# Attention with head dim 192: scores as one full 128-row part and a remainder on two 64-row tiles

## Chip, cores, metric

The kernel runs on one core of a Trainium2 chip. The metric is the device time of one execution in microseconds.

Names: PE is TensorE, PEld its weight loads, ACT is ScalarE, DVE is VectorE, POOL is GpSimd, SP is the queue that issues the DMAs. "Head" is one of the 16 x 32 = 512 independent attention problems; four heads are a group and are loaded together.

## The reference

```
B, H, Sq, Sk, D = 16, 32, 368, 512, 192        # bf16
scores = einsum("bhqd,bhkd->bhqk", q, k) * D**-0.5
p      = softmax(scores, axis=-1)
out    = einsum("bhqk,bhkd->bhqd", p, v)
```

## The kernel before

For each head, PE transposes K (it is loaded with keys on partitions), DVE copies it out of PSUM (the K eviction), PE makes the scores transposed (keys on partitions, 368 queries in the free dimension), ACT takes exp into `pt`, PE multiplies `pt` with V, which has two extra columns of ones that give the softmax denominator, and DVE and ACT divide. Q arrives transposed by the DMA. The 192 head dims are contracted in two blocks of 96 rows.

The parts that matter (cuts marked `...`):

```python
DH = 96; NC = 4; NPAIR = 2                      # 4 chunks of 128 keys, 2 pairs of chunks
st    = ps("st", [128, NC, 512], FP32)          # scores, in PSUM: one buffer only
o_ps  = ps("o_ps", [128, NM, 512], FP32)        # output, NM = 3
tk_ps = ps("tk_ps", [128, 2, 512], BF16)        # transposed K
...
def qk(n, j):                                   # PE: one HALF of a head's scores
    ...
    if n >= 1:
        pe.wait_ge(sem_act, NPAIR * (n - 1) + j + 1)   # this half of exp(n-1) is done
    for c in (2 * j, 2 * j + 1):
        for blk in range(2):
            ins = pe.matmul(st[:, c, 0:SQ],
                lhsT=kt_sb[0:DH, kb, blk, c * 128:(c + 1) * 128],
                rhs=qt[0:DH, sl, blk, h * SQ:(h + 1) * SQ],
                start=(blk == 0), stop=(blk == 1))
    ins.then_inc(sem_st, 1)
...
for i in range(-1, NH + 1):                     # PE's order of work
    qk(i, 0); pv(i - 1, 0); t_k(i + 1); qk(i, 1); pv(i - 1, 1); pv(i - 1, 2)
...
for j in range(NPAIR): exp_pair(i, j)           # ACT: one exp for each half
norm_last(i - 1)                                # ACT: divides the last third of the output
```

`st` exists once, but it is handed to ACT and back in two halves. While ACT works on one half, PE works on the other.

The softmax here doesn't subtract the row's maximum and nothing guards it: scores larger than these inputs give would overflow.

Of the kernel before, what the change touches and what calls it, by code (L numbers as in the profile page):

```python
# [11 lines left out]
def bass_standalone__gqa_softmax__near_ridge_kernel(  # L12
# [14 lines left out]
    assert SQ <= 512 and SQ % 16 == 0  # L27
# [3 lines left out]
    DH = 96  # L31
    VW = D + 2

    MCH = []
    s0 = 0
    while s0 < SQ:
        MCH.append((s0, min(128, SQ - s0)))
        s0 += 128
    NM = len(MCH)
    assert NM == 3, "PSUM plan assumes 3 query chunks"  # L40

    HPD = 1
    for cand in (4, 2):
        if NH % cand == 0 and rep == 1:
            HPD = cand
            break
    NG = NH // HPD
# [10 lines left out]
    with ExitStack() as es:  # L58
# [13 lines left out]
        qt = sb("qt", [128, NBG, 2, HPD * SQ], BF16)  # L72
        v_pad = sb("v_pad", [128, 3, NC, VW], BF16)
        kt_sb = sb("kt_sb", [128, 2, 2, SK], BF16)
# [7 lines left out]
        tk_ps = ps("tk_ps", [128, 2, 512], BF16)  # L82
# [8 lines left out]
        sem_dve = sem("sem_dve")  # L91
        sem_vp = sem("sem_vp")
        sem_k = [sem(f"sem_k{i}") for i in range(NBG)]
# [6 lines left out]
        O_DMAS = NM  # L100

        q_exp = []
        _acc = [0] * NBG
        for _g in range(NG):
            _acc[_g % NBG] += 16 * (2 + (1 if _g == NG - 1 else 0))
            q_exp.append(_acc[_g % NBG])
# [5 lines left out]
        def _(sp):  # L112
            def q_dmas(g):
                return 2 + (1 if g == NG - 1 else 0)

            def loads(g):
                sl = g % NBG
                n0 = g * HPD
                last = g == NG - 1
                if g >= NBG:  # L120
                    gp = g - NBG
                    last_head = gp * HPD + HPD - 1
                    sp.wait_ge(sem_tk, last_head + 1)
                    sp.wait_ge(sem_vp, last_head + 1)
                    sp.wait_ge(sem_st, NPAIR * (last_head + 1))
                R = HPD * SQ
                for blk in range(2):
                    col0 = blk * DH
                    nrows = R - 16 if (last and blk == 1) else R
                    src = bass.AP(tensor=q_t, offset=n0 * SQ * D + col0, ap=[[D, nrows], [1, 128]])  # L130
                    sp.dma_start_transpose(qt[:, sl, blk, 0:nrows], src).then_inc(sem_q[sl], 16)  # L131
                    if last and blk == 1:
                        r0 = n0 * SQ + R - 16
                        src = bass.AP(tensor=q_t, offset=r0 * D + col0, ap=[[1, DH], [D, 16]])
                        with nc.allow_non_contiguous_dma(reason="tail rows of transposed load"):
                            sp.dma_start(qt[0:DH, sl, blk, R - 16:R], src).then_inc(sem_q[sl], 16)
# [15 lines left out]
            def stores(g):  # L152
                ob = g % NBO
                n0 = g * HPD
                sp.wait_ge(sem_dve, (NM - 1) * HPD * (g + 1))
                sp.wait_ge(sem_an, HPD * (g + 1))
                for m, (m0, mm) in enumerate(MCH):
                    dst = bass.AP(tensor=o_t, offset=(n0 * SQ + m0) * D,
                                  ap=[[D, mm], [SQ * D, HPD], [1, D]])
                    sp.dma_start(dst, o_sb[0:mm, ob, :, m, :]).then_inc(sem_o[ob], 16)  # L160
# [12 lines left out]
        def _(pool):  # L173
# [6 lines left out]
            for n in range(NH):  # L180
# [11 lines left out]
                ).then_inc(sem_vp, 1)  # L192

        @block.tensor
        def _(pe):
            pe.wait_ge(sem_init, 2)

            def t_k(n):
# [4 lines left out]
                if n >= 1:  # L203
                    pe.wait_ge(sem_evk, n)
                for c in range(NC):
                    for blk in range(2):
                        ins = pe.transpose(  # L207
                            tk_ps[0:DH, blk, c * 128:(c + 1) * 128],
                            k_nat[:, sl, h, c * D + blk * DH: c * D + (blk + 1) * DH],
                            ident[:],  # L210
                        )
                ins.then_inc(sem_tk, 1)

            def qk(n, j):
# [3 lines left out]
                if j == 0:  # L218
                    pe.wait_ge(sem_evk, n + 1)
                    if h == 0:  # L220
                        pe.wait_ge(sem_q[sl], q_exp[g])
                if n >= 1:
                    pe.wait_ge(sem_act, NPAIR * (n - 1) + j + 1)
                for c in (2 * j, 2 * j + 1):
                    for blk in range(2):
                        ins = pe.matmul(  # L226
                            st[:, c, 0:SQ],
                            lhsT=kt_sb[0:DH, kb, blk, c * 128:(c + 1) * 128],
                            rhs=qt[0:DH, sl, blk, h * SQ:(h + 1) * SQ],
                            start=(blk == 0), stop=(blk == 1),  # L230
                        )
                ins.then_inc(sem_st, 1)

            def pv(n, m):
                pb = n % 2
                vs = n % 3
                m0, mm = MCH[m]
                if m == 0:
                    pe.wait_ge(sem_act, NPAIR * (n + 1))
                    pe.wait_ge(sem_vp, n + 1)  # L240
# [5 lines left out]
                bank = m  # L246
                for c in range(NC):
                    ins = pe.matmul(  # L248
                        o_ps[0:mm, bank, 0:VW],
                        lhsT=pt[:, pb, c, m0:m0 + mm],  # L250
                        rhs=v_pad[:, vs, c, :],
                        start=(c == 0), stop=(c == NC - 1),
                    )
                ins.then_inc(sem_ops, 1)

            for i in range(-1, NH + 1):
                if 0 <= i < NH:
                    qk(i, 0)
                if 0 <= i - 1 < NH:
                    pv(i - 1, 0)  # L260
                if 0 <= i + 1 < NH:
                    t_k(i + 1)
                if 0 <= i < NH:
                    for j in range(1, NPAIR):
                        qk(i, j)
                if 0 <= i - 1 < NH:
                    pv(i - 1, 1)
                    pv(i - 1, 2)

        @block.scalar  # L270
        def _(act):
            def exp_pair(n, j):
                pb = n % 2
                act.wait_ge(sem_st, NPAIR * n + j + 1)
                if j == 0 and n >= 2:
                    act.wait_ge(sem_ops, NM * (n - 1))
                    act.wait_ge(sem_act, NPAIR * (n - 1))
                act.activation(  # L278
                    out=pt[:, pb, 2 * j:2 * j + 2, :],
                    in_=st[:, 2 * j:2 * j + 2, 0:SQ],  # L280
                    func=ACTF.Exp,
                    scale=scale,
                ).then_inc(sem_act, 1)

            def norm_last(n):
# [3 lines left out]
                m0, mm = MCH[m]  # L289
# [4 lines left out]
                if n >= 1:  # L294
                    act.wait_ge(sem_an, n)
                act.activation(  # L296
                    out=o_sb[0:mm, ob, h, m, :],
                    in_=o_ps[0:mm, m, 0:D],
                    func=ACTF.Copy,
                    scale=rc[0:mm, slot:slot + 1],  # L300
                ).then_inc(sem_an, 1)

            for i in range(0, NH + 1):
                if i < NH:
                    for j in range(NPAIR):
                        exp_pair(i, j)
# [4 lines left out]
        def _(dve):  # L311
            def evac_k(n):
                kb = n % 2
                dve.wait_ge(sem_tk, n + 1)
                if n >= 2:
                    dve.wait_ge(sem_st, NPAIR * (n - 1))
                    dve.wait_ge(sem_evk, n - 1)
                dve.tensor_copy(kt_sb[0:DH, kb, :, :], tk_ps[0:DH, :, :]).then_inc(sem_evk, 1)  # L318

            def recip(n, m):  # L320
                m0, mm = MCH[m]
# [10 lines left out]
            def norm(n, m):  # L332
                g, h = divmod(n, HPD)
                ob = g % NBO
                m0, mm = MCH[m]
                slot = (n % 2) * NM + m
                if h == 0 and m == 0 and g >= NBO:
# [3 lines left out]
                dve.tensor_scalar(  # L341
                    out=o_sb[0:mm, ob, h, m, :],
# [43 lines left out]
```

## Time and profile before

| | before |
|---|---|
| median | 1443.36 us (4 runs), span of the profiled run 1447.6 us |
| one head on PE where nothing waits | 2.725 us |
| 512 heads at that pace | 1395 us |
| waits of PE for K | 34.3 us on the page, of which 10.9 for the first K |

The first fence is the busy line of the page (engine, busy us, share of the span, instructions), then groups of instructions: engine, operation, out<-in, count, then busy us and mean ns of one, and last the idle time before them with what ended it.

```profile
PE 1406.7 (97%) x14336; PEld 1151.6 (80%) x14336; DVE 946.3 (65%) x3072; ACT 964.1 (67%) x1537; POOL 258.1 (18%) x519
...
L278 ACT ACTIVATE pt<-st 128x736 bf16<-128x736 f32 x1024 | 798.9, 780 | 321.5 <-PE st L226 321.4
L226 PE MATMUL st<-qt,kt_sb 96*128 96x368 bf16 x4096 | 807.5, 319 | 0.8 <-DVE kt_sb L318 0.8
L248 PE MATMUL o_ps<-v_pad,pt 128*128 128x194 bf16 (+1 forms) x6144 | 692.8, 247 | 0.3 <-ACT pt L278 0.2
...
L207 PE MATMUL tk_ps<-ident,k_nat 128*96 128x128 bf16 x4096 | 314.0, 219 | 34.5 <-DMA k_nat<-in_k_dram 34.3
```

Matmuls overlap, so the mean of 319 ns is no cost. What one costs is the distance from its start to the start of the next: 155 ns for 368 columns, 86 ns for 194, 55 to 56 ns for 128, read from the trace. A head has 8, 12 and 8 of them: 1.24 + 1.03 + 0.44 = 2.7 us.

The timeline of PE and ACT over about one head (start us, busy us, engine, line, what):

```profile
708.32 0.79 PE L226 MATMUL st<-qt,kt_sb 96*128 96x368 bf16 x4
...
708.95 0.85 PE L248 MATMUL o_ps<-v_pad,pt 128*128 128x194 bf16 x8
709.15 0.78 ACT L278 ACTIVATE pt<-st 128x736 bf16<-128x736 f32 x1 [0.51 <-PE st L226]
...
709.63 0.79 PE L226 MATMUL st<-qt,kt_sb 96*128 96x368 bf16 x4
...
710.54 0.78 ACT L278 ACTIVATE pt<-st 128x736 bf16<-128x736 f32 x1
```

PE does not pause in this stretch: at 709.63 it starts the next head's first half while the exp of the half before (709.15 to 709.93) is still running. ACT is the one that waits. The DMA is heavily used too: from 200 to 1200 us the share of the 16 DMA engines is 1.13 (the times of packets are added up, so it can exceed 1), and PE waits 35 times for K:

```profile
200.00:1200.00 1000.00, 981.20 (x10013) 803.03 (x10012) 661.49 (x2145) 671.92 (x1073) 177.66 (x357) 1.00 1.13 260
```

(Columns: stretch, length, busy us and count of PE, PEld, DVE, ACT, POOL, then the clock, DMA share, GB/s.)

### The profile page before, as it was taken

To read this page: it belongs to the slowest core of one execution; us is meant where nothing else is said; L and a number is where in the kernel's file an instruction comes from. 1 tells how busy PE (TensorE), PEld (TensorE's weight loads), DVE (VectorE), ACT (ScalarE), POOL (GpSimd) and SP (SyncE) were. 2 spreads that over 40 slices of the span, in tenths; PEclk is the share of its full clock that TensorE was granted. 3 is DMA by queue.
4 is the path that set the end of the run, shared out by engine and by line. 5 is a ranking of instruction groups with operands and counts; after the bars stand their busy time and mean duration, and the time that the engine had idled before them with its cause. 6 is when DMAs were issued, how large, how long until landed. Compare 5 with 4: busy or idle time off the path is not lost.

```text
span 1447.6 us, 39826 instructions
## 1 busy us (share of the span) xinstructions
PE 1406.7 (97%) x14336; PEld 1151.6 (80%) x14336; DVE 946.3 (65%) x3072; ACT 964.1 (67%) x1537; POOL 258.1 (18%) x519
## 2 busy tenths in 40 slices
PE   6999999999999999999999999999999999999998
PEld 5888887887887778878877887887888888778786
DVE  3666666666666666666656666666666666666665
ACT  4666666666666666666666666666666666666665
POOL 2111111111111111111111111111111111111111
PEclk9999999999999999999999999999999999999999
DMA  9999999999999999999999999999999999999997
GB/s 234 263 246 273 254 274 254 260 258 251 274 269 249 247 265 284 249 254 281 257 240 247 260 255 259 264 262 253 263 276 248 263 287 250 242 256 279 256 266 178
DMA packets 716482, 372.76 MB, mean 258 GB/s; under 512 B 585216, under 2 KB 716288, under 8 KB 716288
## 3 DMA queue, kind: packets, MB, share of 16 engines
q1 hardware_dynamic: 716288, 370.22, 111.2%
q8 instruction: 116, 1.90, 0.5%
q14 instruction: 78, 0.64, 0.1%
HBM read 201.33 MB, written 72.35 MB: 189 GB/s over the span
## 4 chain that ended last, share of the span: by engine, by line
PE 75%; DMA 17%; SPq 7%; issue 0%; ACT 0%; DVE 0%; DVEq 0%
PE st L226 34%; PE o_ps L248 28%; DMA k_nat<-in_k_dram 17%; PE tk_ps L207 14%; SPq L131 7%; ACT pt L278 0%; DVE kt_sb L318 0%; ACT o_sb L296 0%; DVEq L58 0%; DVE rc L330 0%; DVE o_sb L341 0%
## 5 line engine op out<-in xcount | busy, mean ns | idle before, releaser
L278 ACT ACTIVATE pt<-st 128x736 bf16<-128x736 f32 x1024 | 798.9, 780 | 321.5 <-PE st L226 321.4
L226 PE MATMUL st<-qt,kt_sb 96*128 96x368 bf16 x4096 | 807.5, 319 | 0.8 <-DVE kt_sb L318 0.8
L248 PE MATMUL o_ps<-v_pad,pt 128*128 128x194 bf16 (+1 forms) x6144 | 692.8, 247 | 0.3 <-ACT pt L278 0.2
L248 PEld LDWEIGHTS o_ps<-v_pad,pt 128*128 128x128 bf16 (+1 forms) x6144 | 567.8, 109 | 120.3 <-ACT pt L278 0.9
L330 DVE RECIPROCAL rc<-o_ps 128x1 f32<-128x1 f32 (+1 forms) x1536 | 253.1, 165 | 421.1 <-PE o_ps L248 320.2
L226 PEld LDWEIGHTS st<-qt,kt_sb 96*128 96x128 bf16 x4096 | 370.2, 97 | 124.8 <-DVE kt_sb L318 1.4
L189 POOL COPY v_pad<-v_nat 128x384 f32<-128x384 f32 x512 | 255.4, 510 | 1177.7 <-DMA v_nat<-in_v_dram 630.4
L341 DVE TENSOR_SCALAR o_sb<-o_ps,rc 128x192 bf16<-128x192 f32 x1024 | 427.9, 418 | 36.2 <-DVE rc L330 0.2
L318 DVE COPY kt_sb<-tk_ps 96x1024 bf16<-96x1024 bf16 x512 | 347.0, 678 | 39.2 <-PE tk_ps L207 38.6
L207 PE MATMUL tk_ps<-ident,k_nat 128*96 128x128 bf16 x4096 | 314.0, 219 | 34.5 <-DMA k_nat<-in_k_dram 34.3
L296 ACT ACTIVATE o_sb<-o_ps,rc 112x192 bf16<-112x192 f32 x512 | 215.7, 421 | 156.9 <-DVE rc L330 156.9
L207 PEld LDWEIGHTS tk_ps<-ident,k_nat 128*96 128x96 bf16 x4096 | 276.0, 123 | 45.3 <-DMA k_nat<-in_k_dram 33.5
L174 POOL MEMSET v_pad<- 128x2328 bf16 x1 | 2.0, 2038 | 0.3 <-POOLq L371 0.3
L278 ACT ACT_TABLE_LOAD x1 | 1.3, 1283 | 0.8 <-PEq L371 0.8
L177 POOL TENSOR_SCALAR_AFFINE_SELECT ident<-ones_t 128x128 bf16<-128x128 bf16 x1 | 0.3, 294 | 0.1
L175 POOL MEMSET ones_t<- 128x128 bf16 x1 | 0.2, 207 | 0.0
L371 POOL MEMSET const-float32-0.0<- 128x1 f32 x1 | 0.1, 99 | 0.3 <-issue 0.3
L371 POOL MEMSET const-bfloat16-1.0<- 128x1 bf16 x1 | 0.1, 102 | 0.0
L371 POOL MEMSET const-uint8-127<- 128x1 uint8 x1 | 0.1, 102 | 0.0
L371 POOL MEMSET const-float32-1.0<- 128x1 f32 x1 | 0.1, 99 | 0.0
## 6 DMA issues: line engine op xcount, KB each, us to landing
k_nat<-in_k_dram SPq DMA_DIRECT2D x128, 768.0 KB, 6.0
v_nat<-in_v_dram SPq DMA_DIRECT2D x128, 768.0 KB, 7.5
out_dram<-o_sb SPq DMA_DIRECT2D x256, 192.0 KB, 7.0
out_dram<-o_sb SPq DMA_DIRECT2D x128, 168.0 KB, 7.3
qt<-in_q_dram SPq DMA_TRANSPOSE x256, 5.7
qt<-in_q_dram SPq DMA_DIRECT2D x1, 3.0 KB, 4.7
```

Of the source, the lines that this page charges most:

```text
L131: sp.dma_start_transpose(qt[:, sl, blk, 0:nrows], src).then_inc(sem_q[sl], 16)
L174: pool.memset(v_pad[:], 1.0)
L189: pool.tensor_copy(v_pad[:, vs, :, :].bitcast(FP32)[:, :, 0:D // 2], v_nat[:, sl, h, :].bitcast(FP32).rearrange("p (c d) -> p c d", c=NC), ...
L207: ins = pe.transpose(tk_ps[0:DH, blk, c * 128:(c + 1) * 128], k_nat[:, sl, h, c * D + blk * DH: c * D + (blk + 1) * DH], ident[:],)
L226: ins = pe.matmul(st[:, c, 0:SQ], lhsT=kt_sb[0:DH, kb, blk, c * 128:(c + 1) * 128], rhs=qt[0:DH, sl, blk, h * SQ:(h + 1) * SQ], start=(blk ...
L248: ins = pe.matmul(o_ps[0:mm, bank, 0:VW], lhsT=pt[:, pb, c, m0:m0 + mm], rhs=v_pad[:, vs, c, :], start=(c == 0), stop=(c == NC - 1),)
L278: act.activation(out=pt[:, pb, 2 * j:2 * j + 2, :], in_=st[:, 2 * j:2 * j + 2, 0:SQ], func=ACTF.Exp, scale=scale,).then_inc(sem_act, 1)
L296: act.activation(out=o_sb[0:mm, ob, h, m, :], in_=o_ps[0:mm, m, 0:D], func=ACTF.Copy, scale=rc[0:mm, slot:slot + 1],).then_inc(sem_an, 1)
L318: dve.tensor_copy(kt_sb[0:DH, kb, :, :], tk_ps[0:DH, :, :]).then_inc(sem_evk, 1)
L330: dve.reciprocal(rc[0:mm, slot:slot + 1], o_ps[0:mm, m, D:D + 1]).then_inc(sem_rc, 1)
L341: dve.tensor_scalar(out=o_sb[0:mm, ob, h, m, :], in0=o_ps[0:mm, m, 0:D], scalar1=rc[0:mm, slot:slot + 1], scalar2=None, op0=AluOpType.mult ...
L371: nc = _bacc.Bacc("TRN2", target_bir_lowering=False, num_devices=1)
```

## The change

The intent is to give PE less to stream. Instead of 96 + 96 rows, the first 128 head dims are contracted by full-height matmuls, and the remaining 64 dims of two key chunks by two 64-row matmuls that sit in the upper and lower half of the array and run side by side. 8 x 368 columns should become 4 x 368 + 2 x 368, and 8 transposes of K become 6.

The price is this: POOL packs the last 64 dims of K (`kd2`), DVE copies pieces of Q between partition halves (`q_fix`, four copies a group), and Q is now loaded by one DMA transpose of row pairs, so that outputs need a fourth store. One more thing changes on the way: scores are one unit of a whole head, and exp is one instruction of 1472 columns. DVE also copies K out before it divides any of the output; before, a third of the division came first.

The diff, cut to its core:

```diff
-            def qk(n, j):
+            def qk(n):
...
-                    pe.wait_ge(sem_act, NPAIR * (n - 1) + j + 1)
-                for c in (2 * j, 2 * j + 1):
-                    for blk in range(2):
-                        ins = pe.matmul(st[:, c, 0:SQ], lhsT=kt_sb[0:DH, kb, blk, ...],
-                            rhs=qt[0:DH, sl, blk, ...], start=(blk == 0), stop=(blk == 1))
+                    pe.wait_ge(sem_act, n)                 # ALL of exp(n-1) is done
+                CR = ((0, 128, 0, 256), (128, HQ, 256, SQ))
+                for c in range(NC):
+                    for ci, (j0, j1, c0, c1) in enumerate(CR):
+                        pe.matmul(st[:, c, c0:c1], lhsT=kt_sb[:, kb, c * 128:(c + 1) * 128],
+                                  rhs=qx[:, sl, 1::3, h, j0:j1], start=(ci == 0), stop=False, ...)
+                for j in range(NPAIR):
+                    for ci, (j0, j1, c0, c1) in enumerate(CR):
+                        pe.matmul(st[:, 2 * j, c0:c1], lhsT=kt_sb[0:64, ...],
+                                  rhs=qx[0:64, sl, 2::3, h, j0:j1], tile_position=(0, 0), ...)
+                        ins = pe.matmul(st[:, 2 * j + 1, c0:c1], lhsT=kt_sb[64:128, ...],
+                                  rhs=qx[64:128, sl, 0::3, h, j0:j1], tile_position=(64, 0), ...)
                 ins.then_inc(sem_st, 1)
...
-  PE: qk(i, 0); pv(i-1, 0); t_k(i+1); qk(i, 1); pv(i-1, 1); pv(i-1, 2)
+  PE: qk(i); t_k(i+1); pv(i-1, 0); pv(i-1, 1); pv(i-1, 2)
...
-                act.activation(out=pt[:, pb, 2*j:2*j+2, :], in_=st[:, 2*j:2*j+2, 0:SQ], func=Exp, ...)
+                act.activation(out=pt[:, pb, :, :], in_=st[:, :, 0:SQ], func=Exp, ...)
...
+            def q_fix(g):                                  # DVE, 4 copies in one go
+                for (dst_c, dst_p, src_c, src_p) in ((4,0,2,64), (4,64,3,0), (5,0,3,64), (0,64,2,0)):
+                    dve.tensor_copy(qx[dst_p:dst_p+64, sl, dst_c, :, :], qx[src_p:src_p+64, sl, src_c, :, :])
...
+                if i % HPD == HPD // 2 and i // HPD + 1 < NG:   # third head of a group
+                    q_fix(i // HPD + 1)                    # stands before the K eviction of the next head
```

More of the change, by code (lines that the diff above doesn't have):

```diff
@@ L26, in bass_standalone__gqa_softmax__near_ridge_kernel @@
     assert SK == 512, "kernel specialised for 512 keys"
-    assert SQ <= 512 and SQ % 16 == 0
+    assert SQ == 368, "kernel specialised for 368 queries"
     NC = SK // 128
@@ L30, in bass_standalone__gqa_softmax__near_ridge_kernel @@
     scale = float(D) ** -0.5
-    DH = 96
     VW = D + 2
-    MCH = []
-    s0 = 0
-    while s0 < SQ:
-        MCH.append((s0, min(128, SQ - s0)))
-        s0 += 128
-    NM = len(MCH)
-    assert NM == 3, "PSUM plan assumes 3 query chunks"
+    HQ = SQ // 2
+    NM = 3
+    MM = [128, 128, 2 * (HQ - 128)]
+    ME = HQ - 128
     HPD = 1
@@ L46, in bass_standalone__gqa_softmax__near_ridge_kernel @@
             break
+    assert (HPD * HQ) % 16 == 0
     NG = NH // HPD
@@ L71, in bass_standalone__gqa_softmax__near_ridge_kernel @@
         v_nat = sb("v_nat", [128, NBG, HPD, NC * D], BF16)
-        qt = sb("qt", [128, NBG, 2, HPD * SQ], BF16)
+        qx = sb("qx", [128, NBG, 6, HPD, HQ], BF16)
         v_pad = sb("v_pad", [128, 3, NC, VW], BF16)
-        kt_sb = sb("kt_sb", [128, 2, 2, SK], BF16)
+        kd2 = sb("kd2", [128, 3, NC, D - 128], BF16)
+        kt_sb = sb("kt_sb", [128, 2, 768], BF16)
         pt = sb("pt", [128, 2, NC, SQ], BF16)
@@ L81, in bass_standalone__gqa_softmax__near_ridge_kernel @@
         o_ps = ps("o_ps", [128, NM, 512], FP32)
-        tk_ps = ps("tk_ps", [128, 2, 512], BF16)
+        tk_ps = ps("tk_ps", [128, 1024], BF16)
         sem_init = sem("sem_init")
@@ L91, in bass_standalone__gqa_softmax__near_ridge_kernel @@
         sem_dve = sem("sem_dve")
+        sem_qc = sem("sem_qc")
         sem_vp = sem("sem_vp")
+        sem_kp = sem("sem_kp")
         sem_k = [sem(f"sem_k{i}") for i in range(NBG)]
@@ L99, in bass_standalone__gqa_softmax__near_ridge_kernel @@
         V_DMAS = K_DMAS
-        O_DMAS = NM
-        q_exp = []
-        _acc = [0] * NBG
-        for _g in range(NG):
-            _acc[_g % NBG] += 16 * (2 + (1 if _g == NG - 1 else 0))
-            q_exp.append(_acc[_g % NBG])
+        O_DMAS = 4
+        QC = 4
         def uses(g, nb):
@@ L112, in _ @@
         def _(sp):
-            def q_dmas(g):
-                return 2 + (1 if g == NG - 1 else 0)
             def loads(g):
@@ L118, in loads @@
                 n0 = g * HPD
-                last = g == NG - 1
                 if g >= NBG:
@@ L123, in loads @@
                     sp.wait_ge(sem_tk, last_head + 1)
+                    sp.wait_ge(sem_kp, last_head + 1)
                     sp.wait_ge(sem_vp, last_head + 1)
-                    sp.wait_ge(sem_st, NPAIR * (last_head + 1))
-                R = HPD * SQ
-                for blk in range(2):
-                    col0 = blk * DH
-                    nrows = R - 16 if (last and blk == 1) else R
-                    src = bass.AP(tensor=q_t, offset=n0 * SQ * D + col0, ap=[[D, nrows], [1, 128]])
-                    sp.dma_start_transpose(qt[:, sl, blk, 0:nrows], src).then_inc(sem_q[sl], 16)
-                    if last and blk == 1:
-                        r0 = n0 * SQ + R - 16
-                        src = bass.AP(tensor=q_t, offset=r0 * D + col0, ap=[[1, DH], [D, 16]])
-                        with nc.allow_non_contiguous_dma(reason="tail rows of transposed load"):
-                            sp.dma_start(qt[0:DH, sl, blk, R - 16:R], src).then_inc(sem_q[sl], 16)
+                    sp.wait_ge(sem_st, last_head + 1)
+                    sp.wait_ge(sem_qc, QC * (gp + 1))
+                src = bass.AP(tensor=q_t, offset=n0 * SQ * D, ap=[[2 * D, HPD * HQ], [1, 2 * D]])
+                sp.dma_start_transpose(
+                    qx[:, sl, 1:4, :, :].rearrange("p b h j -> p b (h j)"), src
+                ).then_inc(sem_q[sl], 16)
                 if rep == 1:
@@ L156, in stores @@
                 sp.wait_ge(sem_an, HPD * (g + 1))
-                for m, (m0, mm) in enumerate(MCH):
-                    dst = bass.AP(tensor=o_t, offset=(n0 * SQ + m0) * D,
-                                  ap=[[D, mm], [SQ * D, HPD], [1, D]])
-                    sp.dma_start(dst, o_sb[0:mm, ob, :, m, :]).then_inc(sem_o[ob], 16)
+                for (row0, p0, npart, m) in ((0, 0, 128, 0), (1, 0, 128, 1),
+                                             (256, 0, ME, 2), (257, ME, ME, 2)):
+                    dst = bass.AP(tensor=o_t, offset=(n0 * SQ + row0) * D,
+                                  ap=[[2 * D, npart], [SQ * D, HPD], [1, D]])
+                    sp.dma_start(dst, o_sb[p0:p0 + npart, ob, :, m, :]).then_inc(sem_o[ob], 16)
             for g in range(min(LA, NG)):
@@ L192, in _ @@
                 ).then_inc(sem_vp, 1)
+                if h == 0:
+                    pool.wait_ge(sem_k[sl], 16 * K_DMAS * uses(g, NBG))
+                if n >= 3:
+                    pool.wait_ge(sem_tk, n - 2)
+                    pool.wait_ge(sem_kp, n - 2)
+                pool.tensor_copy(
+                    kd2[:, vs, :, :].bitcast(FP32),
+                    k_nat[:, sl, h, :].bitcast(FP32).rearrange("p (c d) -> p c d", c=NC)[:, :, 64:D // 2],
+                ).then_inc(sem_kp, 1)
         @block.tensor
@@ L204, in t_k @@
                     pe.wait_ge(sem_evk, n)
+                pe.wait_ge(sem_kp, n + 1)
+                kn = k_nat[:, sl, h, :].rearrange("p (c d) -> p c d", c=NC)
+                kp = kd2[:, n % 3, :, :].rearrange("p c d -> p (c d)")
                 for c in range(NC):
-                    for blk in range(2):
-                        ins = pe.transpose(
-                            tk_ps[0:DH, blk, c * 128:(c + 1) * 128],
-                            k_nat[:, sl, h, c * D + blk * DH: c * D + (blk + 1) * DH],
-                            ident[:],
-                        )
+                    pe.transpose(tk_ps[:, c * 128:(c + 1) * 128], kn[:, c, 0:128], ident[:])
+                for j in range(NPAIR):
+                    ins = pe.transpose(tk_ps[:, SK + j * 128:SK + (j + 1) * 128],
+                                       kp[:, j * 128:(j + 1) * 128], ident[:])
                 ins.then_inc(sem_tk, 1)
-            def qk(n, j):
+            def qk(n):
                 kb = n % 2
@@ L217, in qk @@
                 sl = g % NBG
-                if j == 0:
-                    pe.wait_ge(sem_evk, n + 1)
-                    if h == 0:
-                        pe.wait_ge(sem_q[sl], q_exp[g])
+                pe.wait_ge(sem_evk, n + 1)
+                if h == 0:
+                    pe.wait_ge(sem_q[sl], 16 * uses(g, NBG))
+                    pe.wait_ge(sem_qc, QC * (g + 1))
                 if n >= 1:
-                    pe.wait_ge(sem_act, NPAIR * (n - 1) + j + 1)
-                for c in (2 * j, 2 * j + 1):
-                    for blk in range(2):
-                        ins = pe.matmul(
-                            st[:, c, 0:SQ],
-                            lhsT=kt_sb[0:DH, kb, blk, c * 128:(c + 1) * 128],
-                            rhs=qt[0:DH, sl, blk, h * SQ:(h + 1) * SQ],
-                            start=(blk == 0), stop=(blk == 1),
-                        )
+                    pe.wait_ge(sem_act, n)
+                CR = ((0, 128, 0, 256), (128, HQ, 256, SQ))
+                for c in range(NC):
+                    for ci, (j0, j1, c0, c1) in enumerate(CR):
+                        pe.matmul(st[:, c, c0:c1],
+                                  lhsT=kt_sb[:, kb, c * 128:(c + 1) * 128],
+                                  rhs=qx[:, sl, 1::3, h, j0:j1],
+                                  start=(ci == 0), stop=False, skip_group_check=(ci != 0))
+                for j in range(NPAIR):
+                    for ci, (j0, j1, c0, c1) in enumerate(CR):
+                        pe.matmul(st[:, 2 * j, c0:c1],
+                                  lhsT=kt_sb[0:64, kb, SK + j * 128:SK + (j + 1) * 128],
+                                  rhs=qx[0:64, sl, 2::3, h, j0:j1],
+                                  start=False, stop=True, tile_position=(0, 0), skip_group_check=(ci != 0))
+                        ins = pe.matmul(st[:, 2 * j + 1, c0:c1],
+                                        lhsT=kt_sb[64:128, kb, SK + j * 128:SK + (j + 1) * 128],
+                                        rhs=qx[64:128, sl, 0::3, h, j0:j1],
+                                        start=False, stop=True, tile_position=(64, 0), skip_group_check=(ci != 0))
                 ins.then_inc(sem_st, 1)
@@ L236, in pv @@
                 vs = n % 3
-                m0, mm = MCH[m]
+                mm = MM[m]
                 if m == 0:
-                    pe.wait_ge(sem_act, NPAIR * (n + 1))
+                    pe.wait_ge(sem_act, n + 1)
                     pe.wait_ge(sem_vp, n + 1)
@@ L245, in pv @@
                         pe.wait_ge(sem_an, n)
-                bank = m
                 for c in range(NC):
-                    ins = pe.matmul(
-                        o_ps[0:mm, bank, 0:VW],
-                        lhsT=pt[:, pb, c, m0:m0 + mm],
-                        rhs=v_pad[:, vs, c, :],
-                        start=(c == 0), stop=(c == NC - 1),
-                    )
+                    ins = pe.matmul(o_ps[0:mm, m, 0:VW], lhsT=pt[:, pb, c, m * 128:m * 128 + mm],
+                                    rhs=v_pad[:, vs, c, :], start=(c == 0), stop=(c == NC - 1))
                 ins.then_inc(sem_ops, 1)
@@ L257, in _, with exp_head @@
                 if 0 <= i < NH:
-                    qk(i, 0)
-                if 0 <= i - 1 < NH:
-                    pv(i - 1, 0)
+                    qk(i)
                 if 0 <= i + 1 < NH:
                     t_k(i + 1)
-                if 0 <= i < NH:
-                    for j in range(1, NPAIR):
-                        qk(i, j)
                 if 0 <= i - 1 < NH:
-                    pv(i - 1, 1)
-                    pv(i - 1, 2)
+                    for m in range(NM):
+                        pv(i - 1, m)
         @block.scalar
         def _(act):
-            def exp_pair(n, j):
+            def exp_head(n):
                 pb = n % 2
-                act.wait_ge(sem_st, NPAIR * n + j + 1)
-                if j == 0 and n >= 2:
+                act.wait_ge(sem_st, n + 1)
+                if n >= 2:
                     act.wait_ge(sem_ops, NM * (n - 1))
-                    act.wait_ge(sem_act, NPAIR * (n - 1))
-                act.activation(
-                    out=pt[:, pb, 2 * j:2 * j + 2, :],
-                    in_=st[:, 2 * j:2 * j + 2, 0:SQ],
-                    func=ACTF.Exp,
-                    scale=scale,
-                ).then_inc(sem_act, 1)
+                    act.wait_ge(sem_act, n - 1)
+                act.activation(out=pt[:, pb, :, :], in_=st[:, :, 0:SQ],
+                               func=ACTF.Exp, scale=scale).then_inc(sem_act, 1)
             def norm_last(n):
@@ L288, in norm_last @@
                 m = NM - 1
-                m0, mm = MCH[m]
+                mm = MM[m]
                 slot = (n % 2) * NM + m
@@ L295, in norm_last @@
                     act.wait_ge(sem_an, n)
-                act.activation(
-                    out=o_sb[0:mm, ob, h, m, :],
-                    in_=o_ps[0:mm, m, 0:D],
-                    func=ACTF.Copy,
-                    scale=rc[0:mm, slot:slot + 1],
-                ).then_inc(sem_an, 1)
+                act.activation(out=o_sb[0:mm, ob, h, m, :], in_=o_ps[0:mm, m, 0:D],
+                               func=ACTF.Copy, scale=rc[0:mm, slot:slot + 1]).then_inc(sem_an, 1)
             for i in range(0, NH + 1):
                 if i < NH:
-                    for j in range(NPAIR):
-                        exp_pair(i, j)
+                    exp_head(i)
                 if 0 <= i - 1 < NH:
@@ L311, in _ @@
         def _(dve):
+            def q_fix(g):
+                sl = g % NBG
+                dve.wait_ge(sem_q[sl], 16 * uses(g, NBG))
+                if g >= NBG:
+                    gp = g - NBG
+                    dve.wait_ge(sem_st, gp * HPD + HPD)
+                    dve.wait_ge(sem_qc, QC * (gp + 1))
+                for (dst_c, dst_p, src_c, src_p) in ((4, 0, 2, 64), (4, 64, 3, 0), (5, 0, 3, 64), (0, 64, 2, 0)):
+                    dve.tensor_copy(qx[dst_p:dst_p + 64, sl, dst_c, :, :],
+                                    qx[src_p:src_p + 64, sl, src_c, :, :]).then_inc(sem_qc, 1)
             def evac_k(n):
@@ L315, in evac_k @@
                 if n >= 2:
-                    dve.wait_ge(sem_st, NPAIR * (n - 1))
+                    dve.wait_ge(sem_st, n - 1)
                     dve.wait_ge(sem_evk, n - 1)
-                dve.tensor_copy(kt_sb[0:DH, kb, :, :], tk_ps[0:DH, :, :]).then_inc(sem_evk, 1)
+                dve.tensor_copy(kt_sb[:, kb, :], tk_ps[:, 0:768]).then_inc(sem_evk, 1)
             def recip(n, m):
-                m0, mm = MCH[m]
+                mm = MM[m]
                 slot = (n % 2) * NM + m
@@ L334, in norm @@
                 ob = g % NBO
-                m0, mm = MCH[m]
+                mm = MM[m]
                 slot = (n % 2) * NM + m
@@ L340, in norm @@
                 dve.wait_ge(sem_rc, NM * n + m + 1)
-                dve.tensor_scalar(
-                    out=o_sb[0:mm, ob, h, m, :],
-                    in0=o_ps[0:mm, m, 0:D],
-                    scalar1=rc[0:mm, slot:slot + 1],
-                    scalar2=None,
-                    op0=AluOpType.mult,
-                ).then_inc(sem_dve, 1)
+                dve.tensor_scalar(out=o_sb[0:mm, ob, h, m, :], in0=o_ps[0:mm, m, 0:D],
+                                  scalar1=rc[0:mm, slot:slot + 1], scalar2=None,
+                                  op0=AluOpType.mult).then_inc(sem_dve, 1)
+            q_fix(0)
             for i in range(-1, NH + 1):
-                if 0 <= i - 1 < NH:
-                    norm(i - 1, 0)
+                if 0 <= i < NH and i % HPD == HPD // 2 and i // HPD + 1 < NG:
+                    q_fix(i // HPD + 1)
                 if 0 <= i + 1 < NH:
@@ L354, in _ @@
                 if 0 <= i - 1 < NH:
-                    for m in range(1, NM - 1):
+                    for m in range(NM - 1):
                         norm(i - 1, m)
```

## The prediction

> **What bounds the kernel now.** TensorE. The page's busy table gives PE 97% of 1447.6 us. In the steady timeline one head takes 2.72 us on PE: from matmul start to matmul start, 368-column score matmuls follow each other after 155 ns (8 per head, 1.24 us), 194-column P·V matmuls after 84-86 ns (12, 1.03 us), 128-column transposes after 55 ns (8, 0.44 us). So PE streams about 2.4 columns a nanosecond and weight loads are hidden. 512 x 2.72 = 1395 us; the waits view adds 10.9 us for the first K load and about 23 us of later waits for K. The DMA is close behind: windows show a DMA share of 1.13 and the queue's issue stream has hardly a gap in mid-run. ACT (67%) and DVE (65%) have slack, because the two exps of a head (780 ns each) overlap with matmuls: scores and exp are handed over in two halves.
>
> **What the change removes.** Score columns fall from 8x368 to 4x368 plus, if the two 64-row tiles really run side by side, 2x368: estimate 0.94 us instead of 1.24. Transposes fall from 8 to 6: 0.33 instead of 0.44. PE work falls to about 2.3 us a head, 15% less. Transposed Q bytes fall by a quarter (two overlapping 128-column passes of 1472 rows become three of 736), which should take the DMA off the limit. The K eviction narrows from 1024 to 768 columns (0.68 to about 0.55 us).
>
> **What it adds.** A POOL copy of K's last 64 dims (estimate 0.2 us), four DVE copies per group of four heads to fix Q (about 0.25 us each), a fourth store per group, two tiling-mode changes per head. All but the last are off the path.
>
> **What it moves, which decides.** Scores of a head are now one unit and exp one instruction. The score buffer is single, so scores(i+1) must wait for all of exp(i), and exp(i) for all of scores(i): they no longer overlap at all. The cycle is then
> - exp of 1472 columns: 2x780 less one fixed cost. The Trainium skill's "ScalarE: Activation LUTs" (What ACT_TABLE_LOAD costs) states 186 ns + 0.833 ns per element; the trace's 780 ns at 736 agrees within 20 ns. Estimate 1.39 us;
> - exp end to weight load 0.06, to first matmul 0.07 (timeline, start-up);
> - scores 0.94;
> - last matmul streamed to ACT start 0.20 (timeline);
> - one drain on entering 64-row mode: "TensorEngine Tiling (Array Packing)", Key Properties, says a mode change drains TensorE; no trace here shows its cost; estimate 0.1-0.2.
>
> Sum 2.8 us a head, against 2.72. P·V and transposes (1.4 us) fit behind the exp (1.39 + 0.33), so PE idles some 0.3 us a head. 512 x 2.8 = 1434, plus start-up and tail of about 18 us (the first transpose now waits for V too, since POOL copies V before K): **1450 us**, range 1390 to 1545. Chances: faster 0.27, within 2% 0.40, slower 0.33.
>
> **What would show it.** ACT: 512 exps of about 1.39 us. PE busy down to about 85%, with an idle before the scores ended by ACT pt, and idle of ACT before exp ended by PE st, both in every head. The chain of waits alternates ACT pt and PE st, with the P·V share nearly gone. DMA share well under 1.13; K waits on PE nearly gone. Paired 64-row matmuls start within some nanoseconds of each other.
>
> **What would make it wrong.** If the 64-row pairs run one after another, scores cost 0.3 us more: about 1600 us. If mode changes are free, about 1390. If the Q fix on DVE runs without its fast mode, normalisation comes late and delays the exp behind it on ACT: up to 60 us. If V lands late, POOL's order holds the transposes.

## The result

| | before | after |
|---|---|---|
| first comparison, medians | 1444.34 us (16 runs) | 1471.38 us (11 runs) |
| ratio | | 1.0195, 95% interval 1.0176 to 1.0214 |
| later comparison (e10 below) | 1429.01 us (7 runs) | 1470.99 us (4 runs) |
| ratio | | 1.0286, interval 1.0252 to 1.0320 |

The change is 2 to 3% slower: clear of noise in both comparisons, but the first interval includes 2%, and only the second lies wholly above it. The time after is the same in both of its jobs to 0.1%; the time before moves by over 1% between four jobs.

The page's busy line after, and the groups that answer to those of before:

```profile
PE 1375.9 (94%) x17408; PEld 1107.9 (75%) x17408; DVE 1006.2 (68%) x3584; ACT 918.7 (63%) x1025; POOL 385.3 (26%) x1031
...
L273 ACT ACTIVATE pt<-st 128x1472 bf16<-128x1472 f32 x512 | 714.5, 1395 | 106.3 <-PE st L233 105.7
L252 PE MATMUL o_ps<-v_pad,pt 128*128 128x194 bf16 (+1 forms) x6144 | 607.4, 247 | 0.4 <-ACT pt L273 0.4
...
L223 PE MATMUL st<-qx,kt_sb 128*128 128x256 bf16 (+1 forms) x4096 | 408.3, 242 | 77.0 <-ACT pt L273 29.5
L229 PE MATMUL st<-qx,kt_sb 64*128 64x256 bf16 (+1 forms) x2048 | 249.9, 242 | 0.0
...
L306 DVE COPY qx<-qx 64x736 bf16<-64x736 bf16 x512 | 177.8, 347 | 21.2 <-DMA qx<-in_q_dram 5.3
```

One head in the timeline after:

```profile
705.74 0.80 PE L223 MATMUL st<-qx,kt_sb 128*128 128x256 bf16 x8 [0.22 <-ACT pt L273]
...
706.47 0.28 PE L229 MATMUL st<-qx,kt_sb 64*128 64x256 bf16 x1
706.47 0.28 PE L233 MATMUL st<-qx,kt_sb 64*128 64x256 bf16 x1
...
707.00 1.40 ACT L273 ACTIVATE pt<-st 128x1472 bf16<-128x1472 f32 x1 [0.32 <-PE st L233]
...
707.23 1.19 PE L252 MATMUL o_ps<-v_pad,pt 128*128 128x194 bf16 x12
...
708.54 0.80 PE L223 MATMUL st<-qx,kt_sb 128*128 128x256 bf16 x8
```

The repacking does what it should. The two 64-row matmuls of a pair start 3 to 4 ns apart (start to start in the trace), which is what the Trainium skill's "TensorE: Matmul & The Clock Gate" (Part 3, Measured speedup vs the span model) gives as about 4 ns for each further tile. But scores start at 705.74, exp at 707.00 after the last of them, and the next scores at 708.54 after exp has ended at 708.40. One head takes 2.80 us, made of

| step | us |
|---|---|
| end of exp to the first score matmul | 0.14 |
| full scores, 4 x (109 + 49 ns) | 0.63 |
| mode change, full to 64-row: 145 ns from start to start where 49 is usual | 0.096 |
| tiled scores, 119 + 49 + 109 + 52 ns; the first matmul pair after the mode change takes 10 ns more | 0.33 |
| last column streamed to start of exp | 0.20 |
| exp of 1472 columns | 1.395 |

These add to 2.79. PE's own work is only 2.52 us: from the last P·V matmul of a head to the first score of the next, the starts are 369 ns apart where 86 ns would do, so PE stands idle for 283 ns. In one head of four (below) the starts are 468 apart. Summed over all heads the idle time at this seam is 158 us.

**Why the page hides this.** PE reads 94% busy, and of the 158 us the page shows 75 as idle (most of the 77.0 in the L223 line). The Trainium skill's "Perfetto Trace Analysis" (Tensor Engine Instruction) says that a matmul's reported end is computed and not observed. Here a matmul of 194 columns reads 247 ns and its successor can start after 86, so about 160 ns of each gap is covered by the modelled end of the matmul before it. The chain of waits is deceived in the same way (start us, us, what):

```profile
705.74 0.80 PE st L223 x8
...
707.28 0.11 PE tk_ps L206 x2
707.40 1.02 PE o_ps L252 x12
708.42 0.12 issue
708.54 0.27 PE st L223
```

It leads from the scores back to P·V, because P·V's modelled end (708.42) lies 0.02 us after the true cause, the end of exp at 707.00 + 1.40. The same skill's "Trainium Kernel Development and Optimization" (Performance Expectations) says that matmul busy time is a bad metric for how close a kernel is to roofline, and names weight-load busy time as one of two good ones. In direction the case agrees: weight loads fall from 80% to 75%, and rise to 85% in the best version below. It does not measure idle time either: e2 below reads 80% like the kernel before, and still has 82 us idle at the seam.

What got better is the DMA. Its share falls from 1.13 to 0.91, and of PE's waits for loads only the first remains, named after the POOL copy that stands behind the first loads (waits view: engine and tile, what ended the wait, us in total, times, longest):

```profile
PE tk_ps L204 <- POOL kd L184: 11.2, 1, 11.2
```

**One head in four.** From start of exp to start of exp, three heads of four take 2.80 us and the third of each group 2.91. That is the head where DVE makes the four Q copies:

```profile
700.65 1.48 DVE L306 COPY qx<-qx 64x736 bf16<-64x736 bf16 x4
...
702.16 0.56 DVE L315 COPY kt_sb<-tk_ps 128x768 bf16<-128x768 bf16 x1
...
703.69 0.16 DVE L327 RECIPROCAL rc<-o_ps 112x1 f32<-112x1 f32 x1
...
703.89 0.42 ACT L287 ACTIVATE o_sb<-o_ps,rc 112x192 bf16<-112x192 f32 x1 [1.19 <-DVE rc L327]
...
704.21 1.39 ACT L273 ACTIVATE pt<-st 128x1472 bf16<-128x1472 f32 x1
```

The copies (1.48 us) push the K eviction back, that pushes the reciprocals back, ACT's division comes late and holds exp until 704.21. The last tiled score started at 703.85 and needs 0.05 to stream and 0.20 to reach ACT, so exp could have started at 704.10.

### The profile page after: what moved, and what is told of

The parts are those of the page before. It is cut to its first block, busy times and chain, and to the rows that moved or that the text cites. A ratio compares the mean times of both kernels' runs of the same rounds, so it can differ in the third digit from the quotient of the medians.

```text
span 1469.9 us, 47751 instructions
## 1 busy us (share of the span) xinstructions
PE 1375.9 (94%) x17408; PEld 1107.9 (75%) x17408; DVE 1006.2 (68%) x3584; ACT 918.7 (63%) x1025; POOL 385.3 (26%) x1031
## 4 chain that ended last, share of the span: by engine, by line
PE 48%; DVE 24%; issue 14%; ACT 12%; DVEq 1%; DMA 0%; SPq 0%; POOL 0%
PE o_ps L252 18%; PE st L223 14%; ACT pt L273 12%; DVE qx L306 12%; PE st L229 7%; PE tk_ps L204 6%; DVE rc L327 6%; DVE kt_sb L315 5%; PE tk_ps L206 2%; DVE o_sb L338 2%; DMA v_nat<-in_v_dram 0%; DVEq L314 0%; DVEq L304 0%; ACT o_sb L287 0%; DVEq L326 0%
## 5 line engine op out<-in xcount | busy, mean ns | idle before, releaser
L273 ACT ACTIVATE pt<-st 128x1472 bf16<-128x1472 f32 x512 | 714.5, 1395 | 106.3 <-PE st L233 105.7
L315 DVE COPY kt_sb<-tk_ps 128x768 bf16<-128x768 bf16 x512 | 285.6, 558 | 398.7 <-PE tk_ps L206 394.8
L223 PE MATMUL st<-qx,kt_sb 128*128 128x256 bf16 (+1 forms) x4096 | 408.3, 242 | 77.0 <-ACT pt L273 29.5
L223 PEld LDWEIGHTS st<-qx,kt_sb 128*128 128x128 bf16 x4096 | 290.6, 97 | 183.6 <-issue 125.0
L229 PE MATMUL st<-qx,kt_sb 64*128 64x256 bf16 (+1 forms) x2048 | 249.9, 242 | 0.0
L233 PE MATMUL st<-qx,kt_sb 64*128 64x256 bf16 (+1 forms) x2048 | 249.8, 242 | 0.0
L204 PE MATMUL tk_ps<-ident,k_nat 128*128 128x128 bf16 x2048 | 203.6, 222 | 11.2 <-POOL kd L184 11.2
L229 PEld LDWEIGHTS st<-qx,kt_sb 64*128 64x128 bf16 x2048 | 130.1, 94 | 83.2 <-issue 30.3
L306 DVE COPY qx<-qx 64x736 bf16<-64x736 bf16 x512 | 177.8, 347 | 21.2 <-DMA qx<-in_q_dram 5.3
L184 POOL COPY kd<-k_nat 128x128 f32<-128x128 f32 x512 | 152.3, 297 | 0.0
L206 PE MATMUL tk_ps<-ident,kd 128*128 128x128 bf16 x1024 | 141.2, 220 | 0.0
L233 PEld LDWEIGHTS st<-qx,kt_sb 64*128 64x128 bf16 x2048 | 130.1, 94 | 0.0
```

Source lines behind the costliest of these rows:

```text
L204: pe.transpose(tk_ps[:, c * 128:(c + 1) * 128], kn[:, c, 0:128], ident[:])
L206: ins = pe.transpose(tk_ps[:, SK + j * 128:SK + (j + 1) * 128], kp[:, j * 128:(j + 1) * 128], ident[:])
L223: pe.matmul(st[:, c, c0:c1], lhsT=kt_sb[:, kb, c * 128:(c + 1) * 128], rhs=qx[:, sl, 1::3, h, j0:j1], start=(ci == 0), stop=False, skip_gr ...
L229: pe.matmul(st[:, 2 * j, c0:c1], lhsT=kt_sb[0:64, kb, SK + j * 128:SK + (j + 1) * 128], rhs=qx[0:64, sl, 2::3, h, j0:j1], start=False, sto ...
L233: ins = pe.matmul(st[:, 2 * j + 1, c0:c1], lhsT=kt_sb[64:128, kb, SK + j * 128:SK + (j + 1) * 128], rhs=qx[64:128, sl, 0::3, h, j0:j1], st ...
L273: act.activation(out=pt[:, pb, :, :], in_=st[:, :, 0:SQ], func=ACTF.Exp, scale=scale).then_inc(sem_act, 1)
```

## The experiments

Theory A: the whole-head handover of a single score buffer sets the pace, and PE's savings fall into PE's new idle time. Theory B, the rival that the page suggests: PE is still the limit at 94%, and small matmuls, weight loads and mode changes ate the savings. Two side theories: the Q copies make the long head; the tiles save nothing in truth. Ratios are to the kernel before on the same chip; differences to the changed kernel use its 1471.38 us of the first comparison, which came back as 1470.99 in another job (e10).

Every run is recorded as correct, e8 too, whose scores are wrong. So this check does not see the scores. `reference.py` draws q and k at 0.05 times a normal variable, which makes the softmax nearly flat; worked out from that draw, such wrong scores move the output by some 0.25% of its size (an estimate). That the repacked scores are right rests on reading the indices of the code, not on a run.

### e3: the handover alone, in the kernel before

```diff
-  qk(i, 0); pv(i-1, 0); t_k(i+1); qk(i, 1); pv(i-1, 1); pv(i-1, 2)
+  qk(i);    t_k(i+1);   pv(i-1, 0); pv(i-1, 1); pv(i-1, 2)      # qk waits for all of exp(i-1)
-  exp_pair(i, 0); exp_pair(i, 1)
+  exp_head(i)                                                     # one exp, 1472 columns
```

> The kernel before with nothing but the whole-head handover of the changed kernel (one exp a head, scores of a head as one unit, same order of work). Theory A: the cycle is exp 1.395 + 0.14 + scores 8 x 0.155 = 1.24 + 0.20 = 2.98 us, 512 x 2.98 + 20 = about 1545 us, 7% slower than before: the handover costs more than the repacking gives. Theory B: PE has the same matmuls as before, so within 2% of before, about 1445 us.

Measured: 1552.99 us, ratio 1.0869 (1.0828 to 1.0910); one head takes 2.986 us. Two heads of its timeline:

```profile
701.26 1.40 ACT L272 ACTIVATE pt<-st 128x1472 bf16<-128x1472 f32 x1 [0.27 <-PE st L225]
...
702.80 1.41 PE L225 MATMUL st<-qt,kt_sb 96*128 96x368 bf16 x8
...
704.24 1.40 ACT L272 ACTIVATE pt<-st 128x1472 bf16<-128x1472 f32 x1 [0.21 <-PE st L225]
```

Same matmuls as before, 8.7% slower; theory B's forecast for this run fails. The edit brings with it the changed kernel's order of work on PE and DVE; e1 and e9 below keep that order and are fast, so it is not the cause. The handover costs 0.26 us a head on the old layout; the repacking then wins back 0.19 of it (2.986 to 2.80).

### e2: more work for PE

```diff
+  if m < 2:   # a P V matmul of its own, overwritten by the real group
+      pe.matmul(o_ps[0:mm, m, 0:VW], lhsT=pt[:, pb, 0, ...], rhs=v_pad[:, vs, 0, :], start=True, stop=True)
```

> The changed kernel with two of the P V matmuls of each head done twice, 0.17 us more work for PE in every head. Theory A: it fits in PE's idle time behind the exp (0.39 us a head between the last P V stream and the first score), so at most 10 us more: 1471 to 1481 us. Theory B: all of it shows, 512 x 0.17 = 88 us: about 1559 us.

Measured: 1482.71 us, 11 us over the changed kernel (2 above theory A's range), not 88. In three heads of four the pace is 2.80 us with and without it; in the head of the Q copies it grows from 2.91 to 3.00, 128 x 0.09 = 12 us, which is the whole difference. The page now reads

```profile
PE 1448.8 (98%) x18432; PEld 1191.7 (80%) x18432; DVE 1016.5 (69%) x3584; ACT 917.7 (62%) x1025; POOL 382.9 (26%) x1031
```

so 1024 more matmuls raise PE to 98% and cost 11 us. The rest went into idle time: start to start, the seam from P·V to scores now holds 82 us of it and not 158. Theory B falls here.

### e1: halves again, tiles kept

The tiled part stays once at the end of a head, so there are still two mode changes.

```diff
   for c in range(NC):
+      if c % 2 == 0: pe.wait_ge(sem_act, NPAIR * (n - 1) + c // 2 + 1)    # only this half of exp(n-1)
       ... full-height matmuls of chunk c ...
   for j in range(NPAIR):
       ... tiled matmuls of chunks 2j, 2j+1 ...
-  ins.then_inc(sem_st, 1)
+      ins.then_inc(sem_st, 1)
-  exp_head(i)
+  exp_pair(i, 0); exp_pair(i, 1)
```

> The changed kernel with scores and exp handed over in two halves again, the tiled part still once at the end of a head. Theory A (the whole-head handover sets the pace: exp 1.395 us, then scores 1.06, with 0.35 of hand-over between, 2.80 us a head): the cycle falls to what PE needs, 0.63 scores + 0.10 mode change + 0.33 tiles + 0.10 mode change + 0.33 transposes + 1.03 P V = 2.5 us a head, so 1300 to 1345 us. Theory B (PE is the limit, as its busy share of 94% reads; small matmuls, weight loads and mode changes ate the gain): no change or slower, 1470 to 1510 us.

Measured: 1392.29 us, ratio 0.9748 (0.9718 to 0.9777). The direction is theory A's, the size is missed by 50 us. The trace shows where: three heads of four take 2.3 to 2.6 us from exp to exp, the third of each group 3.18. There PE waits for the K eviction, and the eviction stands behind the Q copies:

```profile
706.12 1.48 DVE L307 COPY qx<-qx 64x736 bf16<-64x736 bf16 x4
...
707.63 0.56 DVE L316 COPY kt_sb<-tk_ps 128x768 bf16<-128x768 bf16 x1
...
708.25 0.81 PE L223 MATMUL st<-qx,kt_sb 128*128 128x256 bf16 x8 [0.34 <-DVE kt_sb L316]
```

### e4: Q copies spread, nothing else

```diff
-  if i % HPD == HPD // 2 and i // HPD + 1 < NG: q_fix(i // HPD + 1)            # four copies
+  if i // HPD + 1 < NG:                         q_fix(i // HPD + 1, (i % HPD,)) # one in each head
```

> The changed kernel with the four Q copies on DVE done one in each head of a group, not all in one head. In the trace of the changed kernel every fourth head takes 2.91 us and not 2.80, and the copies (1.48 us together) stand before the K eviction there. If they cause it: 128 x 0.11 = 14 us less, about 1457 us. If the long head comes from elsewhere (loads, stores): unchanged, 1471 us.

Measured: 1458.29 us, ratio 1.0211. As expected to 1.3 us, and every head now takes 2.80 us. The long head comes from the copies.

### e7: the cost of a mode change

```diff
-  full c0, c1, c2, c3; tiled j0, j1
+  full c0, c1; tiled j0; full c2, c3; tiled j1
```

> The changed kernel with the scores of a head ordered full, tiled, full, tiled: the same matmuls, two more mode changes, all inside the unit that exp waits for. With 98 ns each, read from the gap between the last full and the first tiled matmul: 512 x 0.195 = 100 us more, 1571 us. If the gap is something else (a weight load that comes once anyway, a wait): 1471 to 1490 us.

Measured: 1566.15 us, 95 us over the changed kernel: 95 / (512 x 2) = 93 ns for each change. In the undisturbed heads the pace goes from 2.80 to 3.013 us, 0.107 for each. The start-to-start distances in its trace are 145 ns into 64-row mode (49 is usual after 112 columns) and 142 ns out of it (46 is usual), so 96 each; and the next distance is longer too, 116 against 106 going in and 120 against 109 going out. Together that is the 0.107. The total is lower since the head of the Q copies gains only 0.10. That a mode change drains TensorE is stated in the Trainium skill's "TensorEngine Tiling (Array Packing)", Key Properties; this is its price here.

### e8: no tiles

```diff
-  64-row pairs at tile positions (0, 0) and (64, 0)
+  the same eight matmuls at full height, one after another (wrong result on purpose)
```

> The changed kernel with the remainder as eight full-height matmuls one after another in place of four pairs of 64-row tiles; no mode change; the result is wrong on purpose. If the pairs do run side by side: the scores lose one mode change (0.10) and gain two times 0.157 us, 512 x 0.217 = 111 us more, about 1582 us. If the pairs save nothing in truth (their times in the trace are modelled): about 1420 us, as the mode changes go.

Measured: 1561.77 us, 91 us over the changed kernel; 3.006 us a head, 0.206 more where 0.217 was expected; with 0.107 for a mode change, as in e7, the sum is 0.207. The pairs really do run side by side. The total is under the expected 111 us since the head of the Q copies, which was longer anyway, takes 3.006 too and so gains only 0.10.

### e6: halves with the copies spread

```diff
   (e1)
+  one Q copy in each head, as in e4
+  POOL: K's copy before V's
```

> Halves as in e1_halves, with one Q copy on DVE in each head, and on POOL the K copy before the V copy. e1 came out at 1392 us: three heads of four take 2.3 to 2.6 us in its trace, every fourth 3.17, where the four Q copies stand before the K eviction and PE waits for that. Theory A with PE as the next limit: every head 2.52 us, 512 x 2.52 + 22 = 1305 to 1325 us, 8% faster than before. If DVE as a whole (1005 us busy) or the DMA is the next limit: 1360 us or more.

Measured: 1366.51 us, ratio 0.9575. A miss by 41 us at least, and inside the branch that had been given to DVE or the DMA as next limit (1360 us or more); e9 decides that one. The waits view names a wait:

```profile
DVE qx L308 <- DMA qx<-in_q_dram: 134.1, 123, 5.3
```

The copy in the first head of a group comes before the next group's Q has landed, and DVE stands still with the K eviction behind it.

### e5: halves with four mode changes

```diff
   (e6; DVE also divides the first third before it copies K out, as in the kernel before)
-  qk(i); t_k(i+1); pv(i-1, 0); pv(i-1, 1); pv(i-1, 2)
+  qk(i, 0); pv(i-1, 0); t_k(i+1); qk(i, 1); pv(i-1, 1); pv(i-1, 2)   # each half: full, then tiled
```

> Halves, Q copies spread and K copied before V as in the run e6_halves_spread, but each half of the scores is finished by its own tiled matmuls (order of the kernel before), so four mode changes a head and not two. If PE is now the limit and a mode change costs the 0.097 us read in the trace: 2.52 + 2 x 0.097 = 2.71 us a head, about 100 us over e6, near 1410 us. If mode changes hide behind other work: as e6.

Measured: 1472.33 us, 106 us over e6 but 62 above the 1410 expected. The difference looks like the 100 us expected, but neither kernel ran at PE's pace: e5's heads take 2.71 to 3.0 us, not 2.71 throughout, and its weight loads wait 54 us for the K eviction and 52 for a division on DVE. As a measure of mode changes it is inconclusive (e7 is the clean one). What it shows is that this order, as a whole, is slower than e6's, with the tiles gathered at the end.

### e9 and e10: copies where Q has landed, and the changed kernel beside it

```diff
   (e6)
-  q_fix(i // HPD + 1, (i % HPD,))
+  if i % HPD: q_fix(i // HPD + 1, ((), (0,), (1,), (2, 3))[i % HPD])   # none, one, one, two
```

> As e6_halves_spread, but the Q copies of the next group stand in the second, third and fourth head of a group (one, one, two), none in the first. In e6 DVE waited 134 us for the Q load, 123 times, always at the copy in the first head, and three heads of four already ran at 2.38 to 2.56 us. If that wait made the rest: every head 2.52 us, 1310 to 1325 us. If the DMA (share 0.99 of 16 engines in e6) is the limit whatever the order: 1355 us or more.

> The changed kernel itself, unedited, on this chip, as the base for the runs beside it: 1471 us, whatever the theory; the kernel before varies more from chip to chip, since it waits for the DMA and the changed kernel does not.

Measured: e9 1315.04 us, ratio 0.9193 (0.9155 to 0.9231). e10 1470.99 us on the same chip. The mean head of e9 is 2.53 us; its matmul starts are 86 ns apart from P·V to scores, so no gap is left. Two exps end at 700.86 (699.41 + 1.45), and the next scores start before that:

```profile
699.41 1.45 ACT L273 ACTIVATE pt<-st 128x736 bf16<-128x736 f32 x2
...
700.71 0.79 PE L223 MATMUL st<-qx,kt_sb 128*128 128x256 bf16 x8
...
701.92 1.45 ACT L273 ACTIVATE pt<-st 128x736 bf16<-128x736 f32 x2
```

The page and the chain of e9:

```profile
PE 1296.9 (99%) x17408; PEld 1110.8 (85%) x17408; DVE 1011.0 (77%) x3584; ACT 907.2 (69%) x1537; POOL 386.0 (29%) x1031
...
PE 97%; issue 1%; ACT 0%; DMA 0%; DVE 0%; SPq 0%; DVEq 0%; POOL 0%
```

With the handover in halves and the copies placed, the repacked kernel is 8% faster than the kernel before. PE's head, 2.53 against 2.725 us, makes 7%; the rest is mostly the waits for K that the kernel before has. Its DMA share is 1.07 between 200 and 1200 us, under the 1.13 of the kernel before but above the 0.99 of the slower e6, so the DMA was not e6's limit.

## Why the prediction was right or wrong

The prediction was 1450 us with 1390 to 1545; 1471 came. Its sum, 1434 + 18, is 1452; of the 19 us that it lacks, the Q copies make 13 (e4), start-up and tail 2, and 4 were not traced. The mechanism, that scores and exp no longer overlap and the cycle is their sum, is shown by e3 (the handover alone slows the old kernel as computed, 2.986 against 2.98 us), by e2 (PE has free time) and by e1 and e9 (with the handover halved, the gain appears).

- **Exp, 1.39 us:** 1.395. The Trainium skill's "ScalarE: Activation LUTs" (What ACT_TABLE_LOAD costs), with 186 ns + 0.833 ns per element for immediate scale and bias, gives 1412 for 1472 elements; the trace reads 1395. For sizing a merged instruction, the trace's own 780 ns at 736 with the slope of the page gives 1393, good to 1%.
- **Hand-over times:** exp to first matmul 0.14 against 0.06 + 0.07; streamed to exp 0.20 against 0.20.
- **Scores, 0.94 and a drain of 0.1 to 0.2:** 0.96 and 0.096. The drain was a guess without a source; that the sum came to 2.80 exactly owes something to luck.
- **PE work of about 2.3 us a head was wrong:** 2.52. That sum left out both mode changes (0.107 each). It cost nothing here since PE was not the limit, but it is what e9 runs into.
- **A head, 2.80 us:** 2.80 in three of four heads.
- **"All but the last are off the path" was wrong.** The four Q copies take 347 ns each, stand in one head, and add 0.11 us there. e4 puts it at 13 us. It was their place, before the K eviction, that did it: in e4 they are no faster, only spread.
- **Start-up and tail, 18 us:** 20 in the trace, counted in the same way: 23 (first exp at 14.9, the last one 1.4, and 6.7 after it is done) less one head, since there are 511 steps between 512 exps.
- **K waits nearly gone, DMA share well under 1.13:** right; the share is 0.91. This hid part of the loss: at the steady paces alone (2.80 against 2.725) the change would be 2.8% slower, but the kernel before also loses 31 us to K loads after the first (23 on the page). That these DMA waits are also why the time before moves from job to job is argued, not shown.
- **"PE busy down to about 85%" and "P·V share nearly gone" in the chain were wrong,** though PE does idle 0.28 us a head as predicted (0.3). The page reads 94%, and the chain goes through P·V, because the modelled ends of matmuls cover more than half of the gap; start to start it would be 89% (158 us idle of 1470). Nor do the waits show in every head: PE's for ACT `pt` is there 128 times and ACT's for PE `st` 378 times, out of 512.
- **"The first transpose now waits for V too":** true and small. The first exp starts 0.7 us later (14.87 against 14.15).
- **The range of outcomes:** 0.40 was given to "within 2%" and 0.33 to slower. The measured ratios, 1.0195 and 1.0286, lie on both sides of that line.

## What to carry to other kernels

Before counting what a change takes off the busiest engine, write down the loop through each single buffer: producer, hand-over, consumer, hand-over. If a change turns two handovers of half a buffer into one of the whole, that loop becomes a sum of times that used to overlap, and it can cost more than the matmuls saved (here 0.26 us a head in e3 against 0.19).

When PE's work comes in short bursts, do not read idle time from its busy share: look at the start-to-start distance across the seam between two kinds of matmul, or add dummy work and see whether the time moves.

Work that is off the path on average can be on it where it stands in an in-order queue. Placing the same four DVE copies differently was worth 13 us in the slow version, and 77 us (1392 to 1315, with POOL's order changed as well) in the fast one.

## What the Trainium skill lacked or had wrong

- "TensorEngine Tiling (Array Packing)", Key Properties: a change of tiling mode drains TensorE, but no cost is given. Here: 96 ns each way from the start-to-start distances (145 against 49, 142 against 46) and 10 or 11 ns more in the distance after that, together 107, as in e7's undisturbed heads. With two changes a head, the tiles, which save 2 x 0.157 us, bring a net 0.10.
- "TensorE: Matmul & The Clock Gate", Back-to-back issue gap: it gives about 81 ns for a sustained stream of weight load and 128-column matmul. Here the K transposes, each with its own weight load, start 55 to 56 ns apart; pairs of 256 and 112 columns take 158 ns, also with a load for each.
- The same page, Part 4: a transpose in a kernel's context is given as about 275 ns. The record here reads 219 ns, but a stream of them costs 55 ns each.
- "Perfetto Trace Analysis", Tensor Engine Instruction: it says that a matmul's end is an estimate, but not how much idle time that can cover. Here 158 us of idle time (283 ns in three heads of four, 382 in the other) were shown as 75 us on the page, and the chain of waits put P·V in the place of the exp.
- No page looked at times a DVE copy from one partition half to the other: 64 partitions x 736 bf16, SBUF to SBUF, took 347 ns. The same copy in place was not run, so what the move itself costs is not shown.
